# A kernel's written-out order of 948 words is replaced by another of 940

## The chip, the cores and the metric

The kernel runs on one core of a Trainium2 chip. The metric is the device time of one execution in microseconds. Before the change it is 148.19 us, the median of three runs (147.37 to 148.43).

## The reference

Four sequences of 768 steps with 8 heads of 48 channels pass through a linear attention whose state decays by w at every step; the result, 3072 rows of 384, goes through a hidden layer of 1024.

```python
for t in range(S):                       # S = 768, for each of 4 x 8 (batch, head)
    cur = outer(u * k[t], v[t])          # 48 x 48
    y[t] = r[t] @ (state + cur)
    state = w[t][:, None] * state + outer(k[t], v[t])
x = y, heads side by side                # 3072 x 384
h = x @ w_in                             # 3072 x 1024
solu = h * softmax(h)
ln = (solu - mean) / sqrt(var + 1e-6) * g_ln
out = ln @ w_out                         # 3072 x 384
```

## The kernel before

**Tiling.** Steps are cut into 6 chunks of 128. A unit is one chunk of one sequence with all 8 heads; units 0 to 3 are the first chunk of the four sequences, unit 23 is the last. A unit's state depends on the unit four before it.

**One unit.** Four loads of 192 KB bring w, k, r and v (`LW`, `LK`, `LR`, `LV`; functions `load_w` to `load_v`, lines 263 to 273). `lw` takes the logarithm of w on ACT, `cum` sums it along time with two products on PE, `ex` makes exponentials on ACT in place, and `kp` multiplies them with k and r on DVE. `krk` and `krr` turn the scaled k and r by four transposes each on PE, and `kr` copies them out of PSUM; or `kt` (line 398) turns both by one DMA transpose on SP. `M` are the scores, `m` their copy (DVE with the mask, or ACT, and then `sel` masks on GpSimd). `p`, `q`, `qh`, `dg`, `dv` make the bonus of the current step: products on GpSimd (`p` = k r, `q` = p u, `dv` = v dg) and a sum on DVE (`dg`). `vb` casts v. `Y` is the attention's result, `y` its copy; `S`, `et`, `st` carry the state on. `X` turns y by three transposes on PE and `xT` copies it, or `xt` (line 401) does both by DMA. `H` is the hidden product, `e` its exponential on ACT, `he` the product of both on DVE, `hq` its square on ACT, `ea` the sum of the two halves of e on GpSimd. `Oa` and `Ob` are the first and second half of the output product, with one column for the mean and one-column products for the sums of e (of `ea`, if the unit has it) and of hq. `sq`, `qm`, `lv`, `rs` make the scale, `o` applies it, `out` stores 192 KB.

**By rows.** A unit that has the word `ht` (line 404) lays its hidden layer out by rows: six matmuls of 512 columns instead of 24 of 128, sums by the engines' accumulators (two more short readings on ACT and one short square, `sv`) instead of one-column products, and a DMA transpose that turns `he` back. The last unit does its hidden layer in two halves (`HA` to `QB`).

**Weights.** `LI` and `LO` load w_in (three parts of 512 KB) and w_out (two of 768 KB); `wi` casts, `gw` multiplies by g_ln, `mn` makes the column mean, and `ce` subtracts it. `H` needs the first, `Oa` all of them. `hot` issues products of no use that keep PE warm.

**What sets the order.** The string `ORDER` (lines 21 to 68) is the whole schedule. Each word is one stage of one unit, and what follows the dot is an engine (a: ACT, d: DVE, p: GpSimd, which the profile calls POOL), a PSUM bank, or for a load the queue that issues it (none: SP, a: ACT, g: GpSimd). The words are issued from left to right, and `InOrder` (line 73) ties each instruction to the one before it on its engine. So each engine runs its own words in the order of the string and waits where an operand isn't there; between engines nothing is fixed but data. SP is one such queue: a store that waits for `o` or a transpose that waits for `kp` holds up all loads behind it. Buffers come in rings: 7 of each input, 10 of lw and vb, 6 of kp, kr and dv, 4 of most others; a load of unit i waits until unit i - 7 is used.

```python
    for word in ORDER.split():
        word, _, how = word.partition(".")
        name = word.rstrip("0123456789")
        stages[name](int(word[len(name):]), how)
```

All instructions are recorded under line 89, that of the helper, and so are told apart by their tiles.

Of the kernel before, what the change touches and what calls it, by code (L numbers as in the profile page):

```python
# [18 lines left out]


ORDER = """
LR2.a LW0.a LW5 LW2 LV2.g LU0.a LW1.a LK2 LK0.a LW4 LR5 LK5 LV6.g lw2 hot10.0 cum2.0 lw0 cum0.6 LV3.g us0.3
lw5 ex2 kp2 LG0.a ik0 LR0.a cum5.0 uc0 krk2.2 LK1.a LV5.g ih0 ex0 LR1.a krr2 p2 kr2.d q2 qh2 p0 hot3.3 M2.2 q0
LK4 LR4 ex5 dg2 m2.d lw1 hot4.4 cum1.4 LV0.a kp0 vb2.a hot1.2 S2.2 dv2 krk0.3 p5 dg0 p1 lw4 ex1 LW3 cum4.6 kp5
LW6 vb0.p gs0.0 LV1.a dv0 q1 et2 kp1 krr0 ex4 LR3.a kr0.d krk1.1 krr1 LK3.a gc0 kp4 st2 M0.3 kr1.a lw3 vb6.a
LO0.a m0.d hot1.5 M1.6 krk4.2 krr4 LR6 LK6 Y2.i5 vb1.a q5 cum3.3 m1.d lw6 qh1 S1.0 krk5.1 vb5.a cum6.6 dg1
kr4.d S0.2 et1 ex3 ex6 LI0.a kp3 LO1 et0 y2.a krr5 LV4.g LW7 LR7 p3 Y0.i4 dv1 q3 qh3 p4 Y1.n3 y0.a st1 st0
krk3.0 hot1.2 M4.4 kr5.d p6 q4 vb4.p krr3 vb3.a LW8 LK7 kp6 y1.d hot1.1 X1.6 kr3.a LI1.a wi0.p m4.d gw2.a
gw0.a gw1.a dg3 LI2.a gw3.a krk6.0 X2.2 krr6 xT2.d S3.7 et3 gw4.a S5.4 xT1.d dv3 M5.2 S4.1 kr6.d gw6.a et4
M3.5 m5.d q6 X0.0 gw5.a M6.2 et5 xT0.a gw7.a wi1.a m3.d st4 LV8.g wi2.a mn0.5 qh5 lw7 dg4 Y3.i0 dv4 st3 m6.d  # L30
y3.a mc0 dg5 ce2.d ce5.d st5 ce4.d H1.6 LV7.g X3.3 ce7.d xT3.d e1 H0.0 cum7.2 LK8 LW11 LW9 LV9.g he1 lw8 H3.4
e0 he0 H2.6 ex7 e3 S6.0 ce3.p LR11 kp7 he3 ce1.p LR8 ce0.p hq0.a krk7.3 ce6.p Y4.n1 e2 hq1.a et6 ea0.p ea3.p
krr7 y4.d dv5 he2 lw11 st6 Oa0.2 cum8.4 ex8 Ob0 ea1.p kr7.d sq0 LR9 cum11.6 X4.0 ex11 p8 LK11 LR10 qm0 lv0
Oa1.1 lw9 Y5.i3 p7 kp8 rs0 LK10 LW10 M7.4 q7 Ob1 xT4.d kp11 hq3.a y5.a sq1 krk8.0 krk11.6 vb8.p o0.d dg6 LK9
m7.a X5.7 LW12 qm1 krr11 out0 lv1 ea2.p LR12 lw10 vb7.p cum9.2 LV11 xT5.d sel7 q8 dg7 kr11.d rs1 o1.d ex9 krr8
kp9 lw12 H5.4 cum10.6 kr8.d ex10 Oa3.1 p10 e5 hq2.a dv6 kp10 H4.2 cum12.6 Ob3 he5 out1 LK12 dg8 Oa2.0 ex12 sq3
dv7 qm3 e4 p9 vb9.p LV12 lv3 hq5.a ea4.p kp12 S8.4 he4 krk10.5 q9 et8 rs3 Ob2 sq2 M8.6 krr10 LW14 LR14 Y7.n3
vb11.p krk12.2 dv8 o3.d LK14 qm2 lw14 m8.a lv2 st8 S7.1 krk9.4 cum14.6 LW13 y7.d krr12 krr9 kr10.d rs2 out3
et7 vb12.p p11 st7 o2.a ex14 Y6.n0 hq4.a S9.1 et9 kr9.d Oa4.5 q11 LK17 out2 kp14 M9.3 M10.6 Ob4 LW17 kr12.a
LW15 X7.2 sel8 st9 ea5.p y6.d S11.0 m9.a m10.d p12 sq4 xT7.a qm4 M11.3 lv4 M12.1 LR17 et11 rs4 dg9 dv9 sel9  # L40
lw17 Y8.n6 Oa5.7 LV10 m11.d o4.a st11 LK15 cum17.4 Ob5 m12.a y8.d ex17 q10 X6.3 sq5 dg11 vb10.p lw13 q12 qm5
out4 xT6.a lv5 lw15 kp17 LK13 rs5 krk14.0 S12.1 X8.6 xT8.d krr14 LR13 o5.a dg10 cum13.2 LR15 dv11 et12 H6.4
kr14.d out5 st12 ex13 cum15.6 e6 LW16 p14 H7.0 kp13 p13 dv10 ex15 he6 LV15 ea6.p H8.2 LK16 kp15 e7 S10.4 Y9.n5
hq6.a he7 krk15.7 Y10.n6 LW18 lw16 LV16 e8 krr15 et10 y9.d y10.d LR16 M14.0 sel12 Oa6.5 he8 vb15.p X9.6 Ob6
m14.a xT9.d ea7.p LW21 hq7.a sq6 q13 lw18 kr15.d cum16.2 st10 Y11.n6 H9.0 qm6 y11.d M15.6 dg12 ex16 ea8.p
Oa7.4 lv6 rs6 o6.a e9 p15 qh13 LR18 dv12 q14 kp16 LK18 hq8.a m15.d krk16.2 X11.3 vb16.a Ob7 krr16 sq7 he9
cum18.5 q15 p16 out6 dg13 qm7 ex18 p18 lv7 Y12.n7 LK21 LW19 Oa8.0 X10.1 rs7 o7.a y12.d lw21 LR21 kp18 Ob8
xT10.d ea9.p sq8 xT11.d X12.4 S15.7 cum21.5 LK20 out7 lw19 qm8 xT12.d lv8 dg15 dg14 rs8 dv15 q16 ex21 H11.3
# [622 lines left out]
```

## Time and profile before

| | |
|---|---|
| median of 3 runs | 148.19 us |
| profiled execution | 148.38 us |
| its span, first to last instruction | 146.7 us |
| mean granted clock of PE | 0.976 |
| HBM read and written | 22.03 MB, 4.72 MB |
| DMA, mean over the span | 208 GB/s |
| first cumulative sums on PE | 6.17 us |
| last weight landed | 33.3 us |
| first half of the first output | 42.7 us |
| last PE instruction ended | 142.1 us |

The profile is of one execution. Busy shares are those of each engine (PE is TensorE's products, PEld its weight loads); where a line gives a wait, it names what ended it. Small differences between times in the trace are good to a few hundredths of a microsecond, sums of means to about one.

### The profile page before, as it was taken

How to read it: one execution, taken by the hardware profiler on the slowest of the kernel's cores; microseconds unless marked ns; L12 is line 12 of the kernel's file. 1: busy time of each engine (PE TensorE's matmuls, PEld its weight loads, DVE VectorE, ACT ScalarE, POOL GpSimd, SP SyncE). 2: the span in 40 equal slices, each digit the busy share in tenths (PEclk: the TensorE clock that was granted, in tenths of full speed). 3: DMA queues.
4: the chain of work that ended last, by engine and by line, in shares of the span. 5: the costliest groups of instructions: out<-in, count | busy, mean ns of one | idle time of the engine just before them, and what ended most of it. 6: DMA issues, size and time to landing. Idle time of an engine off the chain costs nothing.

```text
span 146.7 us, 4751 instructions
## 1 busy us (share of the span) xinstructions
PE 129.6 (88%) x1847; PEld 96.0 (65%) x1851; DVE 122.5 (84%) x221; ACT 121.9 (83%) x262; POOL 117.7 (80%) x153
## 2 busy tenths in 40 slices
...
GB/s 94 282 295 259 259 261 399 350 352 202 250 173 187 162 222 211 220 203 198 219 138 244 178 243 164 221 189 206 204 182 167 153 197 117 210 190 112 206 107 107
DMA packets 111160, 30.56 MB, mean 208 GB/s; under 512 B 106265, under 2 KB 110370, under 8 KB 111138
## 3 DMA queue, kind: packets, MB, share of 16 engines
...
q10 hardware_dynamic: 12418, 4.53, 11.4%
q0 software_dynamic: 512, 1.57, 3.4%
q8 instruction: 14, 0.23, 0.6%
q14 instruction: 8, 0.07, 0.1%
HBM read 22.03 MB, written 4.72 MB: 182 GB/s over the span
## 4 chain that ended last, share of the span: by engine, by line
PE 33%; DMA 27%; ACT 15%; DVE 10%; POOL 6%; issue 6%; SPq 2%; DVEq 0%; ACTq 0%
PE ps L89 33%; DMA wout_f<-in_moe_w_out_dram 7%; DMA w_in<-in_w_dram 6%; DMA v_in<-in_v_dram 6%; DMA kr_in<-in_k_dram 5%; DVE kp L89 3%; DMA kr_in<-in_r_dram 3%; DVE he L89 2%; ACT ps L89 2%; POOL ea L89 2%; SPq L89 2%; ACT o L89 2%; ACT w L89 1%; POOL m L89 1%; ACT e L89 1%
## 5 line engine op out<-in xcount | busy, mean ns | idle before, releaser
L89 PE MATMUL ps<-w,he 128*128 128x385 bf16 x192 | 43.0, 325 | 0.1
L89 DVE TENSOR_TENSOR kp<-ps,kr_in 128x768 bf16<-128x768 f32 x24 | 22.8, 952 | 6.8 <-ACT ps L89 6.2
L89 PE MATMUL ps<-xT,win_sb 128*128 128x128 bf16 x456 | 28.3, 219 | 0.2 <-ACT win_sb L89 0.2
L89 PEld LDWEIGHTS <-win_sb 128*128 128x128 bf16 x456 | 26.3, 98 | 2.9 <-issue 1.5
L89 ACT ACTIVATE e<-ps 128x1024 bf16<-128x1024 f32 (+1 forms) x25 | 24.5, 985 | 1.6 <-PE ps L89 1.5
L89 PE MATMUL ps<-one_col,hq 128*128 128x1 bf16 x152 | 25.0, 164 | 0.6 <-ACT et L89 0.5
L89 POOL TENSOR_TENSOR p<-kr_in 128x384 bf16<-128x384 f32 x24 | 23.7, 1000 | 1.8 <-DMA kr_in<-in_r_dram 1.7
L89 POOL TENSOR_TENSOR ea<-e 128x512 bf16<-128x512 bf16 x18 | 20.8, 1153 | 5.4 <-ACT e L89 5.4
L89 DVE TENSOR_TENSOR he<-ps,e 128x1024 bf16<-128x1024 f32 (+1 forms) x20 | 23.0, 1164 | 1.4 <-ACT e L89 1.4
L89 ACT ACTIVATE ps<-ps 128x768 f32<-128x768 f32 x24 | 19.3, 805 | 3.3 <-PE ps L89 1.8
L89 POOL TENSOR_TENSOR q<-p,u_bc 128x384 bf16<-128x384 bf16 x24 | 21.7, 911 | 0.3
L89 PEld LDWEIGHTS <-he 128*128 128x128 bf16 x192 | 18.0, 96 | 5.9 <-DMA he<-win_f 0.6
L89 POOL TENSOR_TENSOR dv<-vb,dg 128x384 bf16<-128x384 bf16 x24 | 19.9, 831 | 0.7 <-DVE dg L89 0.4
L89 DVE TENSOR_TENSOR m<-ps,keep 128x1024 bf16<-128x1024 f32 x16 | 19.3, 1218 | 1.1 <-PE ps L89 1.0
L89 ACT ACTIVATE hq<-he 128x1024 bf16<-128x1024 bf16 x18 | 19.0, 1053 | 0.0
L89 PEld LDWEIGHTS <-kp 128*128 128x128 bf16 x208 | 13.8, 102 | 3.0 <-issue 0.6
L89 PEld LDWEIGHTS <-hq 128*128 128x128 bf16 x152 | 11.4, 96 | 6.3 <-ACT hq L89 0.7
L89 ACT ACTIVATE lw<-w_in 128x384 bf16<-128x384 f32 x24 | 12.4, 523 | 3.7 <-DMA w_in<-in_w_dram 3.7
L89 PEld LDWEIGHTS <-kr 64*128 64x128 bf16 (+1 forms) x272 | 10.7, 97 | 6.3 <-issue 2.9
L89 DVE TENSOR_REDUCE dg<-q 128x8 f32<-128x384 bf16 (+1 forms) x24 | 11.4, 478 | 2.9 <-POOL q L89 1.9
L89 PE MATMUL ps<-ident,kp 128*128 128x128 bf16 x128 | 12.7, 234 | 0.2 <-DVE kp L89 0.2
L89 PE MATMUL ps<-inv_col,ea 128*128 128x1 bf16 x72 | 11.9, 165 | 0.0
...
## 6 DMA issues: line engine op xcount, KB each, us to landing
...
```

The costliest lines, as they stand in the source:

```text
L89: made = make(*args, **kwargs)
```

## The change

Only the string `ORDER` changes: the engines, the banks and the places of the words. The code of the stages stays. Counted by words:

| | before | after |
|---|---|---|
| loads of v issued by GpSimd | 8 | 11 (units 10, 11, 12 added) |
| k and r turned by DMA (`kt`) | 8 units: 13, 17 to 23 | 10: 12, 13, 15, 17 to 23 |
| y turned by DMA (`xt`) | unit 23 | 16, 19, 20, 23 |
| hidden layer by rows, turned by DMA (`ht`) | 17 to 21 | 18, 20, 21 |
| `kr` copies on DVE, ACT | 13, 3 | 11, 3 |
| `xT` copies on DVE, ACT | 16, 7 | 13, 7 |
| `o` on DVE, ACT | 11, 13 | 13, 11 |
| `vb` on GpSimd, ACT | 14, 10 | 15, 9 |
| `ea` on GpSimd | 18 | 16 |
| `gw` on ACT, GpSimd | 8, 0 | 7, 1 |
| `ce` on DVE, GpSimd | 4, 4 | 3, 5 |
| warm-up products of `hot` | 21 | 32 |
| u loaded by | ACT | SP |

Which units take which of two engines changes for other words too, without changing the counts (`m` with `sel`, `y`, `wi`, `qh`), and the banks and the order are others throughout. Shown are the start, the lines with the added GpSimd loads, and the stretch from `Ob9` to the end:

```diff
--- before.py
+++ after.py
@@ -19,52 +19,50 @@
 
 
 ORDER = """
-LR2.a LW0.a LW5 LW2 LV2.g LU0.a LW1.a LK2 LK0.a LW4 LR5 LK5 LV6.g lw2 hot10.0 cum2.0 lw0 cum0.6 LV3.g us0.3
-lw5 ex2 kp2 LG0.a ik0 LR0.a cum5.0 uc0 krk2.2 LK1.a LV5.g ih0 ex0 LR1.a krr2 p2 kr2.d q2 qh2 p0 hot3.3 M2.2 q0
-LK4 LR4 ex5 dg2 m2.d lw1 hot4.4 cum1.4 LV0.a kp0 vb2.a hot1.2 S2.2 dv2 krk0.3 p5 dg0 p1 lw4 ex1 LW3 cum4.6 kp5
-LW6 vb0.p gs0.0 LV1.a dv0 q1 et2 kp1 krr0 ex4 LR3.a kr0.d krk1.1 krr1 LK3.a gc0 kp4 st2 M0.3 kr1.a lw3 vb6.a
...
-et15 o8.d kp21 hq9.a kr16.d e11 H12.0 e12 LV14 LW20 st15 H10.5 q18 he11 Oa9.2 Y15.n7 out8 LV13 Ob9 ea11.p he12
-kt13 vb14.a e10 LK19 hq11.a qh16 sq9 he10 lw20 qm9 lv9 vb13.p y15.d Oa11.4 rs9 o9.a p17 M16.0 hq12.a LV17 dv13
-ea12.p M13.5 Ob11 sel14 m13.d X15.2 LR19 sq11 S13.7 Y13.n3 q17 xT15.a cum19.5 qm11 out9 ea10.p lv11 Oa12.2
-rs11 et13 m16.d o11.a y13.d st13 S14.1 ex19 et14 LR20 kp19 dv14 Ob12 X13.7 S16.0 cum20.4 hq10.a LW22 st14 dg18
-p19 Y14.n1 out11 xT13.a sq12 p20 kt18 et16 kt17 lw22 qm12 lv12 st16 rs12 o12.a dg16 out12 H13.6 ex20 dv16 e13
-p21 y14.d vb17.a dg17 kp20 Y16.n1 H15.2 e15 LW23 he13 Oa10.5 LK22 q20 X14.4 y16.d xT14.d Ob10 he15 hq13.a sq10
-S17.4 M17.6 M18.0 lw23 qm10 et17 H14.2 dv17 lv10 rs10 ea13.p st17 m17.a X16.4 LV19 q19 o10.d hq15.a e14 sel17
-LR22 LV18 m18.d out10 Oa13.7 ea15.p xT16.d LK23 LR23 vb18.p he14 cum22.0 q21 ex22 H16.5 Ob13 Y17.n4 Oa15.2 e16
-dv18 kp22 cum23.0 he16 y17.d vb19.a S19.3 hq14.a kt19 dg20 LV20 Y18.n6 qh21 sq13 X17.5 ex23 qm13 kp23 ea14.p
-kt20 qh19 Ob15 y18.d xT17.a lv13 M19.4 kt21 vb20.a sq15 rs13 p23 dg21 H17.0 qm15 o13.a m19.d et19 X18.7 st19
-Oa14.6 M20.4 lv15 p22 e17 out13 xT18.d ea16.p rs15 dg19 S18.3 Ob14 m20.a sq14 he17 dv20 LV21 M21.4 sel20 o15.d
-qm14 kt22 m21.d H18.0 hq16.a dv19 vb21.p Y20.n2 lv14 et18 rs14 dv21 Y19.n7 st18 kt23 q22 q23 y20.d o14.a y19.d
-out14 out15 e18 Oa16.4 Y21.n3 X19.7 X20.6 he18 hq17.a xT20.d Ob16 M22.0 sq16 xT19.a M23.5 LV22 y21.d m22.d
-m23.a qm16 H20.2 X21.5 e20 dg22 vb22.p dv22 xT21.d lv16 sv17 sel23 LV23 H19.6 vb23.p ht17 dg23 Y22.n5 sv18
-ht18 H21.0 dv23 he20 y22.d Oa17.2 rs16 e19 he19 sv20 Y23.n3 hq20.a o16.d hq18.a Ob17 e21 sq17 Oa18.7 X22.4
-hq19.a y23.d xT22.d qm17 ht20 Ob18 sq18 he21 H22.3 qm18 lv17 rs17 lv18 ht19 o17.d rs18 o18.d Oa20.0 e22 xt23
-out16 hq21.a Oa19.1 Ob20 sq20 ht21 he22 qm20 sv21 ea22.p HA23.5 Ob19 lv20 sv19 rs20 hq22.a out18 sq19 EA23
-o20.d qm19 lv19 rs19 HB23.4 out17 DA23 o19.a out20 QA23.d Oa21.2 EB23 Oa22.6 Ob21 Oa23.1 sq21 Ob22 qm21 DB23
-lv21 QB23.d rs21 o21.a out19 out21 sq22 qm22 Ob23 lv22 sq23 qm23 rs22 lv23 rs23 o22.d o23.a out22 out23
+LV6.g LW0.a LR2.a LW2 LU0 LW5 LK0.a LV3.g lw0 LV2.g hot10.0 cum0.1 LK2 LR0.a lw2 LW3 LG0.a LR3.a hot1.0 cum2.3 ex2
+ik0 LV4.g us0.0 ex0 uc0 kp2 LV5.g p2 hot5.5 krk2.6 krr2 LW1.a kp0 q2 lw3 gs0.4 hot1.0 cum3.2 LK3.a lw5 gc0 LK1.a
+kr2.d p0 M2.5 dg2 cum5.0 krk0.4 ex5 LK5 vb2.p dv2 krr0 LR5 m2.d kr0.d ih0 q0 kp5 hot2.5 M0.6 Y2.i4 ex3 LW4 LR1.a
+kp3 lw1 dg0 m0.d LR4 LK4 hot2.0 cum1.0 krk5.5 vb5.p krr5 krk3.2 y2.a krr3 X2.3 kr5.d vb3.a xT2.d kr3.d LV1.a ex1
+vb4.a lw4 LV0.a hot3.4 cum4.6 LW6 LO0.a kp1 p3 LK6 p5 hot3.4 M3.2 q5 ex4 p1 S2.4 krk1.0 vb1.a lw6 krr1 q1 kp4 kr1.a
+m3.d krk4.1 q3 qh1 LI2.a krr4 dg3 dg1 hot1.5 M1.5 vb0.a S1.0 p4 et2 cum6.2 q4 dv0 m1.d hot2.7 S0.6 et1 dv1 ex6
...
+et5 gw2.a wi2.a m5.d st0 dg4 y3.d dg5 xT0.a gw6.a M4.4 gw1.a hot1.2 S4.3 LW8 dv5 y1.d dv4 wi1.p X1.2 m4.d xT1.d
+krk6.0 LK8 krr6 LV7.g gw7.p S3.7 S6.5 et4 LK7 gw5.a gw0.a et3 LV10.g wi0.a LV9.g LW7 LR8 X3.2 kr6.d st5 Y5.i4 gw4.a
+st4 LV8.g st3 M6.0 Y4.i3 et6 H0.6 m6.d xT3.d mn0.0 st6 y4.a y5.a lw8 e0 cum8.2 X5.1 lw7 mc0 ex8 ce0.d ce7.d cum7.4
...
+p10 he2 cum11.3 kr8.d qm0 dv6 lv0 lw9 rs0 kp10 sq3 LR9 dg7 krk7.1 Oa1.5 cum9.6 krr7 qm3 o0.d Ob1 ex11 LV11.g kp11
...
+dg9 out2 LV12.g xT6.a sq4 lw15 kt12 qm4 lv4 ea5.p rs4 st7 X7.5 LR15 H6.3 xT7.d et8 dg11 o4.d vb9.p ex14 p12 q12
...
+dg15 he12 hq11.a S13.4 q18 Oa9.7 cum19.0 M13.5 Ob9 ex19 vb14.a S15.3 sq9 m13.d et13 qm9 st13 LW22 q17 LK19 kp19
+dv15 kt17 Oa11.2 ea12.p Y13.n6 lv9 p19 LW20 et15 y13.d LR21 Y15.n5 y15.d Ob11 S14.1 rs9 dv14 LV17 o9.a out9 hq12.a
+sq11 qm11 lw21 st15 lv11 LV16 ea10.p X13.5 vb17.p rs11 o11.d hq10.a xT13.d lw20 dg17 LK21 sel16 out11 M17.6 Y14.n0
+Oa12.4 X15.5 Ob12 vb16.p cum21.2 m17.a y14.d dg16 H13.6 sq12 dg18 lw22 dv17 Oa10.0 dv16 qm12 ex21 sel17 kt18 et14
+st14 X14.1 lv12 e13 Ob10 kp21 q19 xT15.a ea13.p rs12 M18.2 xT14.a he13 LV18 sq10 LK20 o12.d S17.5 Y17.n1 cum20.6
+m18.a sel18 LR20 Y16.n4 qm10 lv10 y17.d LK22 et17 rs10 H15.2 vb18.p dv18 o10.d ex20 cum22.0 hq13.a y16.d st17 H14.4
+kp20 S16.6 e15 LW23 ex22 he15 p20 q20 LR22 out12 kp22 qh20 Oa13.7 lw23 e14 out10 xt16 hq15.a cum23.2 Ob13 p21 et16
+sq13 he14 qm13 LR23 Y18.n0 y18.d X17.1 xT17.d H16.4 st16 LK23 ex23 hq14.a kp23 e16 H17.0 lv13 ea15.p ea14.p q21
+LV20 he16 X18.2 Oa14.6 LV19 rs13 e17 vb20.a kt19 Oa15.3 p23 ea16.p hq16.a Ob14 M19.4 o13.d sq14 Ob15 vb19.p dg20
+kt21 kt20 he17 qm14 lv14 q23 xT18.d rs14 o14.a hq17.a m19.d sq15 dv20 dg21 out13 dg19 Oa16.0 M21.1 M20.4 m20.d kt22
+ea17.p kt23 m21.a qm15 H18.6 e18 dv19 lv15 p22 Y19.n1 y19.d sel21 out14 q22 Y20.n4 LV21 y20.d rs15 Oa17.2 he18
+vb21.p LV23 Ob16 xt19 dv21 o15.a sq16 Ob17 qm16 dg23 lv16 rs16 sq17 M23.3 qm17 M22.6 LV22 m23.d o16.a S18.1 Y21.n5
+vb22.p lv17 rs17 vb23.a m22.a hq18.a y21.d S19.0 out15 H19.3 xt20 sel22 et18 dv23 et19 o17.d X21.2 sv18 H20.5 out16
+dg22 ht18 st19 e19 xT21.a out17 st18 Y23.n7 H21.1 he19 y23.d dv22 xt23 e20 ea19.p Oa18.4 he20 hq19.a Y22.n0 e21
+Ob18 Oa19.3 y22.d hq20.a ht20 X22.0 Ob19 he21 sq18 sv20 xT22.a qm18 lv18 ht21 H22.0 rs18 HA23.5 Oa20.2 sq19 qm19
+lv19 rs19 o18.d sv21 o19.d e22 he22 EA23 hq21.a hq22.a Oa21.3 out18 Ob20 sq20 ea22.p DA23 Ob21 qm20 QA23.d HB23.1
+lv20 Oa22.4 sq21 rs20 EB23 qm21 Oa23.6 lv21 out19 rs21 Ob22 o21.a sq22 o20.d DB23 QB23.d qm22 Ob23 out20 lv22 rs22
+sq23 out21 qm23 lv23 o22.d out22 rs23 o23.a out23
 
 NIO, NLW, NKP, NWK, NHT = 7, 10, 6, 4, 4
```

More of the change, by code (lines that the diff above doesn't have):

```diff
@@ L21 @@
 ORDER = """
-LR2.a LW0.a LW5 LW2 LV2.g LU0.a LW1.a LK2 LK0.a LW4 LR5 LK5 LV6.g lw2 hot10.0 cum2.0 lw0 cum0.6 LV3.g us0.3
-lw5 ex2 kp2 LG0.a ik0 LR0.a cum5.0 uc0 krk2.2 LK1.a LV5.g ih0 ex0 LR1.a krr2 p2 kr2.d q2 qh2 p0 hot3.3 M2.2 q0
-LK4 LR4 ex5 dg2 m2.d lw1 hot4.4 cum1.4 LV0.a kp0 vb2.a hot1.2 S2.2 dv2 krk0.3 p5 dg0 p1 lw4 ex1 LW3 cum4.6 kp5
-LW6 vb0.p gs0.0 LV1.a dv0 q1 et2 kp1 krr0 ex4 LR3.a kr0.d krk1.1 krr1 LK3.a gc0 kp4 st2 M0.3 kr1.a lw3 vb6.a
-LO0.a m0.d hot1.5 M1.6 krk4.2 krr4 LR6 LK6 Y2.i5 vb1.a q5 cum3.3 m1.d lw6 qh1 S1.0 krk5.1 vb5.a cum6.6 dg1
@@ L27 @@
[L27 to L46, printed above, removed]
@@ L47 @@
-cum18.5 q15 p16 out6 dg13 qm7 ex18 p18 lv7 Y12.n7 LK21 LW19 Oa8.0 X10.1 rs7 o7.a y12.d lw21 LR21 kp18 Ob8
-xT10.d ea9.p sq8 xT11.d X12.4 S15.7 cum21.5 LK20 out7 lw19 qm8 xT12.d lv8 dg15 dg14 rs8 dv15 q16 ex21 H11.3
-et15 o8.d kp21 hq9.a kr16.d e11 H12.0 e12 LV14 LW20 st15 H10.5 q18 he11 Oa9.2 Y15.n7 out8 LV13 Ob9 ea11.p he12
-kt13 vb14.a e10 LK19 hq11.a qh16 sq9 he10 lw20 qm9 lv9 vb13.p y15.d Oa11.4 rs9 o9.a p17 M16.0 hq12.a LV17 dv13
-ea12.p M13.5 Ob11 sel14 m13.d X15.2 LR19 sq11 S13.7 Y13.n3 q17 xT15.a cum19.5 qm11 out9 ea10.p lv11 Oa12.2
@@ new lines @@
+vb4.a lw4 LV0.a hot3.4 cum4.6 LW6 LO0.a kp1 p3 LK6 p5 hot3.4 M3.2 q5 ex4 p1 S2.4 krk1.0 vb1.a lw6 krr1 q1 kp4 kr1.a
+m3.d krk4.1 q3 qh1 LI2.a krr4 dg3 dg1 hot1.5 M1.5 vb0.a S1.0 p4 et2 cum6.2 q4 dv0 m1.d hot2.7 S0.6 et1 dv1 ex6
+Y1.n7 st2 st1 dv3 M5.4 Y0.i0 LI1.a et0 LR6 kp6 gw3.a qh4 vb6.a kr4.a Y3.n3 LO1 hot1.2 S5.1 y0.a LI0.a X0.0 p6 q6
+et5 gw2.a wi2.a m5.d st0 dg4 y3.d dg5 xT0.a gw6.a M4.4 gw1.a hot1.2 S4.3 LW8 dv5 y1.d dv4 wi1.p X1.2 m4.d xT1.d
+krk6.0 LK8 krr6 LV7.g gw7.p S3.7 S6.5 et4 LK7 gw5.a gw0.a et3 LV10.g wi0.a LV9.g LW7 LR8 X3.2 kr6.d st5 Y5.i4 gw4.a
```

14 lines of the change are left out of this document (added).

## The prediction

> **What bounds the kernel now.** I read the page's busy times first, then the stages, the waits, the timeline of the late part, and only then the groups for prices.
>
> ```profile
> PE 129.6 (88%) x1847; PEld 96.0 (65%) x1851; DVE 122.5 (84%) x221; ACT 121.9 (83%) x262; POOL 117.7 (80%) x153
> ```
>
> No engine stands out over the span. The stages 28 to 88, 88 to 118 and 118 us to the end (busy us of PE, PEld, DVE, ACT, POOL; clock; DMA share; GB/s) say more:
>
> ```profile
> 28.00:88.00 60.00, 57.07 (x946) 46.96 (x944) 58.28 (x99) 57.22 (x115) 57.22 (x68) 1.00 0.97 215
> 88.00:118.00 30.00, 28.07 (x453) 21.54 (x451) 25.92 (x43) 26.25 (x57) 26.21 (x30) 1.00 0.99 184
> 118.00:147.00 29.00, 23.89 (x280) 15.83 (x280) 20.34 (x38) 22.60 (x63) 9.73 (x12) 0.99 0.63 155
> ```
>
> In the first stage DVE, ACT and POOL are each 95 to 97% busy: three engines bound at once, and a saving on one alone moves nothing. In the second each loses about 4 us. In the third PE works nearly without a gap until 142.1 us, and POOL has little left. What opens the 4 us is in the waits (total, times, longest):
>
> ```profile
> POOL vb L89 <- DMA v_in<-in_v_dram: 4.5, 2, 2.9
> ACT vb L89 <- DMA v_in<-in_v_dram: 1.5, 1, 1.5
> ```
>
> and in POOL's and PE's timeline (start, duration; in brackets the idle time before and what ended it):
>
> ```profile
> 91.05 0.50 POOL L89 CAST vb<-v_in 128x384 bf16<-128x384 f32 x1 [1.57 <-DMA v_in<-in_v_dram]
> 126.48 0.50 POOL L89 CAST vb<-v_in 128x384 bf16<-128x384 f32 x1 [2.93 <-DMA v_in<-in_v_dram]
> 115.99 0.33 PE L89 MATMUL ps<-ident,y 128*128 128x128 bf16 x3 [1.05 <-ACT o L89]
> ```
>
> v arrives late because SP, one in-order queue, stands behind stores that wait for o:
>
> ```profile
> SPq L89 <- ACT o L89: 6.7, 7, 1.5
> SPq L89 <- DVE o L89: 6.6, 6, 1.9
> ```
>
> So: before 28 us DMA arrival bounds (27 loads of units 0 to 6 land 0.75 us apart until 22.6 us, the weights until 33.3); then three engines together; from about 88 us SP's late loads; from 116 us PE.
>
> **The change, part by part.** Prices, from the groups (count, busy us, mean ns):
>
> ```profile
> L89 POOL TENSOR_TENSOR ea<-e 128x512 bf16<-128x512 bf16 x18 | 20.8, 1153 | 5.4 <-ACT e L89 5.4
> L89 POOL DMA_DIRECT2D v_in<-in_v_dram x8 | 7.4, 923 | 0.0
> L89 POOL TENSOR_TENSOR w<-w,mean_sb 128x384 bf16<-128x384 bf16 x4 | 3.3, 870 | 0.0
> L89 ACT ACTIVATE o<-ps,rs 128x384 f32<-128x384 f32 x13 | 7.5, 580 | 0.3
> L89 ACT ACTIVATE w<-wout_f,gr 128x384 bf16<-128x384 f32 x8 | 4.5, 611 | 0.1
> L89 DVE COPY kr<-ps 128x1024 bf16<-128x1024 bf16 x13 | 8.9, 683 | 1.0 <-PE ps L89 1.0
> L89 DVE COPY xT<-ps 128x384 bf16<-128x384 bf16 x16 | 5.4, 350 | 0.6 <-PE ps L89 0.5
> L89 DVE TENSOR_SCALAR o<-ps,rs 128x384 f32<-128x384 f32 x11 | 6.8, 614 | 0.8 <-ACT rs L89 0.6
> kr<-kp SPq DMA_TRANSPOSE x8, 4.2
> ```
>
> *POOL.* Two `ea` fewer, -2 x 1.153; three loads more, +3 x 0.923; a cast of v, +0.502; a `ce`, +0.870; a `gw`, which POOL has never done here. That one lies between the cast (0.50, one f32 input of the same shape) and `p` (1.00, two); I take 0.6, by the cast. Sum -2.31 + 2.77 + 0.50 + 0.87 + 0.6 = **+2.4 us** (2.3 to 2.8). Counted by words, 1.0 of it stands before Ob16, the 17th second half of an output; the rest lies behind, where POOL has time.
>
> *ACT.* Two `o` (-1.16), a `gw` (-0.61), a cast (-0.51) and two units less by rows, each of which reads two accumulators and squares one column (-2 x (0.200 + 0.196 + 0.191) = -1.17): **-3.4 us**. *DVE.* Two `kr` (-1.37), three `xT` (-1.05), one `ce` (-0.61), two `o` more (+1.23): **-1.8 us**. What is late once they are faster is POOL, which feeds dv, q and the cast v to both: of a saving of 2 to 3 us I count 0.8, between nothing and all of it.
>
> *PE.* 16 + 9 transposes less, 0.056 us from start to start: -1.4. One-column products: 16 of hq and 32 of e more, 8 of ea less, 40 x 0.026 (the step behind each in the timeline): +1.0. Two units' hidden products by 24 matmuls of 128 columns (1.34) for 6 of 512 (1.30): +0.1. Eleven more warm-up products in the start, where PE waits for loads: nothing, at most 11 x 0.24 = 2.6 if they came when work is ready. The total is level, but its place isn't: behind Ob16 the new order has S18, S19 and Y21 (0.46, 0.46, 0.37) and a net -0.15 of other work: **+1.1 us** in the stage in which PE is full.
>
> *The start.* Unit 0's r is the 10th load rather than the 14th, so kp0 starts near 10 us, not at 12.9; but unit 5's is now the 19th, at 4 + 17 x 0.75 = 16.8 us, and kp5 started at 15.4. Units 0 to 6 are the same 28 loads. All weights are queued ahead of units 7 and 8, where w7, r7 and w8 came between: up to -3 x 0.75 = -2.2 us for the last weight, but the new order puts H0 behind S6, Y4 and Y5, by its engines' sums at about the old time. I take -0.3, ends -2 and +1.
>
> *SP.* Three v loads leave (0.62 each, median), u's load comes, and transposes go from 14 to 17, at 1.8 us each from the late ones (14.2 us for eight): +4 us over the span. Queued behind each transpose and store are the next loads, for which POOL (v, k, r), ACT (w, v) and DVE (k, r) wait. From Ob9 to Ob16 SP had 14 loads, 8 transposes, 7 stores; it gets 19, 8 and 6: **+2.5 us** of issue in the very stage where v is late. The cover is slack: SP waits 13.3 us for o in all. With it nothing, without it 2.5. In the forecast I leave it at nothing, since 13.3 us is the larger number. A moved transpose replaces some 0.44 us of PE and 0.68 of DVE by 4.2 us of latency from issue to landing; every one has its own product ordered 2 us or more behind it, by the engines' sums, so that it too is SP's matter.
>
> *The three GpSimd loads.* By the engines' sums, units 10 and 11 are queued 16 to 18 us ahead of their casts and unit 12 some 5 us, so their landing (4.9 us) is covered; what they cost is POOL's 0.923 us each. [...]
>
> **Sum.** POOL paces to Ob16: +1.0; PE from there: +1.1; start -0.3; relief -0.8: **+1.0 us**. The profiled execution took 148.38 us (span 146.7 and 1.7 around it), 0.2 over the median of 148.19. Forecast **149.4 us**, own range 148.0 to 151.0 from the starts' ends, POOL's and half the SP bound. Under 1% (1.5 us) this kernel's measurement can't tell from no change.
>
> **Rivals.**
>
> *Relief decides (0.26).* If ACT and DVE, not POOL, pace the middle, their savings count. Up to Ob16 ACT's words sum to 4.5 us less, DVE's to 2.2 less (part of it moved behind); with +1.1 for PE that is -3.4 or -1.1, and with the start 144.7 or 147.0; I take 145.9. For it: ACT and DVE were as busy as POOL. Against: POOL's idle time in 28 to 88 us is 2.8, a third of it one wait for a weight, and it gets more to do. It decides once POOL has more than 1.0 us to spare before Ob16.
>
> *SP's loads come later (0.25), slower.* One mechanism: in the stretch Ob9 to Ob16 the five added loads put SP 2.5 us later, v and k, r land late by that, and POOL and then PE stand. It decides from the point at which SP's waits for o fall under 2.5 us there. 149.4 + 2.5 = 151.9. For it: v is already late by 1.6, 1.5 and 2.9 us. Against: SP still waits for o in that stage.
>
> [...]
>
> *Nothing moves (0.07).* The orders differ but the same arrivals and the same total of PE (-0.3) decide: 148.2.
>
> **How the numbers follow.** Forecast 0.40: of it 0.23 within 1%, 0.16 slower, 0.01 faster. Relief: 0.24 faster, 0.02 within. SP and GpSimd: 0.27 slower. Nothing moves: 0.06 within, 0.01 faster. Faster 0.26, same 0.31, slower 0.43. The range reaches from the middle of the relief case to just over the SP case: 145.2 to 152.6.
>
> **What would show it.** Right: POOL busy near 120 us with under 3 us idle between 28 and 88; ACT near 118.5, DVE near 120.7; the 17th output's second half ending about a microsecond later; PE full from there. POOL's `gw` row gives the unseen price. The relief case would show POOL waiting for ACT less than the 5.4 us of `ea<-e`, and Ob16 by 120 us. The SP case would show waits of `vb` for v_in above 6 us in sum and POOL idle over 4 us in 88 to 118. I am wrong altogether if the start moves by more than 2 us: then kp6 no longer starts near 26 us.

## The result, and the profile after

The new order is slower: 153.84 us median of 4 runs (152.48 to 155.25), against 148.31 (147.37 to 149.08) for before beside it; the ratio is 1.0346, 95% interval 1.0245 to 1.0446. The profiled execution took 153.94 us (span 152.2), 5.6 more than the one of before. The experiments ran on several chips, on which before's own median lay between 147.92 and 149.64 us, so they are compared by their ratio to before on the same chip; 0.01 is 1.5 us. Executions in a slower state of the chip are left out of the ratios, among them after's of 155.25 us, three of start_of_after's four and the profiled one of before_fill.

The busy times of after (all instructions stand under the helper's line, 89 in before, 87 in after, 88 in some experiments):

```profile
PE 133.5 (88%) x1913; PEld 98.8 (65%) x1913; DVE 121.3 (80%) x217; ACT 121.1 (80%) x252; POOL 120.7 (79%) x157
```

The stages 28 to 88, 88 to 118 and 118 us to the end (columns as before: PE, PEld, DVE, ACT, POOL, clock, DMA share, GB/s):

```profile
28.00:88.00 60.00, 56.00 (x896) 46.15 (x896) 54.95 (x93) 54.91 (x109) 55.69 (x67) 0.97 0.94 209
88.00:118.00 30.00, 28.40 (x469) 22.64 (x467) 25.73 (x44) 27.08 (x54) 27.58 (x32) 1.00 0.97 190
118.00:153.00 35.00, 27.14 (x364) 18.77 (x362) 22.49 (x40) 24.58 (x65) 14.24 (x17) 0.97 0.59 145
```

Two things stand out. In the first stage every engine has lost 1.1 to 3.3 us of busy time and the granted clock reads 0.97 where it read 1.00. In the last stage TensorE is idle for 7.9 of 35 us (5.1 of 29 in before); 5.3 and 4.9 of these lie behind its last product, so while it has work it stands for some 2.6 us against 0.2. The waits (total, times, longest):

```profile
POOL ea L87 <- ACT e L87: 8.8, 3, 5.8
POOL vb L87 <- DMA v_in<-in_v_dram: 6.3, 3, 2.5
PE ps L87 <- DMA kr<-kp: 2.4, 3, 1.1
SPq L87 <- DVE o L87: 13.9, 6, 5.9
SPq L87 <- ACT o L87: 2.5, 7, 0.6
```

and the groups that answer to the prices of the prediction:

```profile
L87 POOL DMA_DIRECT2D v_in<-in_v_dram x11 | 10.1, 920 | 0.0
L87 POOL TENSOR_SCALAR w<-wout_f,gr 128x384 bf16<-128x384 f32 x1 | 1.3, 1268 | 0.0
```

**Where the 5.6 us went.** A word of the order has a price on TensorE: its matmuls, each at its usual time from one start to the next, which is short of its length in the timeline because matmuls overlap (in after the 24 of H0, 0.22 us long each, take 1.35 us from the first one's start at 35.28 us to the next word's at 36.63). Take the start of a word and subtract the prices of all words ahead of it on TensorE (warm-ups not counted): that is TensorE's lag, the time that it has stood or run slowly so far. The differences between the columns are what counts; with the median of these times they come out the same to 0.1 or 0.2 us, while the columns themselves move by up to 0.9. From the two traces, and from two of the experiments below, in us:

| at (us) | before | after | he0_first | four_pe |
|---|---|---|---|---|
| 38 | 20.3 | 21.1 | 21.2 | 20.8 |
| 46 | 21.5 | 25.0 | 22.7 | 22.2 |
| 102 | 24.1 | 26.2 | 25.1 | 24.0 |
| 118 | 25.7 | 28.7 | 26.4 | 26.5 |
| 134 | 26.1 | 32.0 | 29.3 | 27.0 |

After loses 3.5 us against before up to 46 us, of it 2.7 between 38 and 46; it wins 1.4 back up to 102; and loses 3.8 again behind 102 us, 2.9 of them between 118 and 134. So there are two losses at two places and a gain between them.

**The first place.** The timelines of TensorE and DVE in after (start, length; in brackets the idle time ahead):

```profile
41.03 5.81 PE L87 MATMUL ps<-xT,win_sb 128*128 128x128 bf16 x72 [2.11 <-DVE he L87]
```

```profile
38.71 1.14 DVE L87 SCALAR_TENSOR_TENSOR w<-wout_f,gr,ps 128x384 bf16<-128x384 f32 x2 [1.86 <-ACT mean_sb L87]
39.76 1.22 DVE L87 TENSOR_TENSOR he<-ps,e 128x1024 bf16<-128x1024 f32 x1
```

H3 goes into the bank of H0, which he0 has to read first. On DVE he0 stands behind two centrings (ce0, ce7), and these wait 1.86 us for the mean, which ScalarE copies at 38.16 us, behind an exponential and a logarithm. TensorE stands for 2.11 us. What follows is in the stages of 3.41 us around it (TensorE's busy time, clock, DMA share, GB/s):

```profile
38.14:41.55 3.41, 1.30 (x17) 1.00 1.14 290
41.55:44.96 3.41, 3.41 (x36) 0.50 0.97 195
44.96:48.37 3.41, 3.41 (x56) 1.00 1.06 209
```

Right behind the gap the clock reads 0.50 for 3.41 us, and the 72 matmuls of H3, H1, H2 take 5.81 us.

**The second place.** Three of TensorE's waits between 92 and 136 us; in before TensorE has no wait for kr, xT or vb there:

```profile
PE ps L87 <- DMA kr<-kp: 1.9, 2, 1.1
PE ps L87 <- DMA xT<-y: 0.9, 1, 0.9
PE ps L87 <- POOL vb L87: 0.7, 1, 0.7
```

The waits for kr are those of the scores of units 18 and 19, and these two are turned by DMA in before as well. Their sources were ready at 83.1 and 95.9 us (83.5 and 96.8 in before), but SP came to kt18 at 101.2 and to kt19 at 114.0 us, 5.2 and 5.9 us later than in before, while TensorE itself was 2 to 3 us behind. Only the wait for xT, 0.9 us ahead of H20, is the landing of a transpose that the change had added; vb is GpSimd's cast of v21.

Two theories were set against each other. S+L (its second half is Theory SP further on): the loss at the start is he0's wait and the clock, the late loss is SP's list. Rival P, later Rival A: the engines' pace sets the end wherever one begins, so neither matters. The results, ratio to before and interval:

| kernel | ratio | interval |
|---|---|---|
| after | 1.0346 | 1.0245 to 1.0446 |
| start_of_before | 1.0454 | 1.0382 to 1.0526 |
| late_of_before | 1.0615 | 1.0558 to 1.0673 |
| he0_first | 1.0197 | 1.0139 to 1.0255 |
| warm_fill | 1.0167 | 1.0096 to 1.0237 |
| tail_order | 1.0254 | 1.0182 to 1.0325 |
| tail_pe | 1.0162 | 1.0085 to 1.0238 |
| tail_both | 1.0171 | 1.0065 to 1.0277 |
| out_later | 1.0116 | 1.0032 to 1.0200 |
| all_pe | 1.0124 | 1.0042 to 1.0205 |
| after_late_g | 1.0139 | 1.0074 to 1.0205 |
| all_pe_late_g | 1.0273 | 1.0203 to 1.0343 |
| four_pe | 1.0069 | 1.0019 to 1.0119 |
| four_pe_stores | 1.0141 | 1.0072 to 1.0209 |
| before_turned | 1.0665 | 1.0553 to 1.0776 |
| before_loads_g | 1.0026 | 0.9971 to 1.0081 |
| before_fill | 1.0095 | 1.0047 to 1.0143 |
| before_late_g | 1.0003 | 0.9954 to 1.0052 |

### The profile page after: what moved, and what is told of

It is laid out like the page before. It is cut to its first block, busy times and chain, and to the rows that moved or that the text cites. A ratio compares the mean times of both kernels' runs of the same rounds, so it can differ in the third digit from the quotient of the medians.

```text
span 152.2 us, 4862 instructions
## 1 busy us (share of the span) xinstructions
PE 133.5 (88%) x1913; PEld 98.8 (65%) x1913; DVE 121.3 (80%) x217; ACT 121.1 (80%) x252; POOL 120.7 (79%) x157
## 3 DMA queue, kind: packets, MB, share of 16 engines
q0 software_dynamic: 704, 2.16, 4.9%
## 4 chain that ended last, share of the span: by engine, by line
PE 49%; DMA 25%; DVE 12%; SPq 4%; ACT 3%; POOL 2%; issue 2%; ACTq 0%; DVEq 0%; POOLq 0%
PE ps L87 49%; DMA w_in<-in_w_dram 7%; DMA kr<-kp 7%; DMA v_in<-in_v_dram 6%; SPq L87 4%; DVE kp L87 4%; DMA kr_in<-in_r_dram 3%; DVE m L87 3%; DMA xT<-y 2%; DVE he L87 2%; DVE dg L87 1%; POOL vb L87 1%; POOL dv L87 1%; DVE kr L87 1%; ACT ps L87 1%
## 5 line engine op out<-in xcount | busy, mean ns | idle before, releaser
L87 PE MATMUL ps<-xT,win_sb 128*128 128x128 bf16 x504 | 32.5, 225 | 2.5 <-DVE he L87 2.5
L87 PEld LDWEIGHTS <-win_sb 128*128 128x128 bf16 x504 | 30.5, 101 | 3.9 <-issue 2.9
L87 DVE TENSOR_TENSOR he<-ps,e 128x1024 bf16<-128x1024 f32 (+1 forms) x22 | 25.7, 1171 | 3.1 <-ACT e L87 3.1
L87 PE MATMUL ps<-one_col,hq 128*128 128x1 bf16 x168 | 27.5, 164 | 0.0
L87 POOL TENSOR_TENSOR ea<-e 128x512 bf16<-128x512 bf16 x16 | 18.5, 1157 | 8.8 <-ACT e L87 8.8
L87 ACT ACTIVATE hq<-he 128x1024 bf16<-128x1024 bf16 x20 | 21.0, 1052 | 1.0 <-DVE he L87 0.9
L87 PEld LDWEIGHTS <-hq 128*128 128x128 bf16 x168 | 13.3, 96 | 6.9
L87 DVE TENSOR_TENSOR y<-ps,dv 128x384 bf16<-128x384 f32 x20 | 10.7, 551 | 2.6 <-PE ps L87 1.3
L87 POOL CAST vb<-v_in 128x384 bf16<-128x384 f32 x15 | 7.5, 503 | 6.3 <-DMA v_in<-in_v_dram 6.3
L87 PE MATMUL ps<-ident,kp 128*128 128x128 bf16 x112 | 9.8, 226 | 2.5 <-POOL p L87 1.9
```

Source lines behind the costliest of these rows:

```text
L87: made = make(*args, **kwargs)
```

## Experiments: the two orders spliced

Each takes the words of one order up to a point and what is then missing in the order of the other.

```diff
 start_of_before: 308 words of before (to cum10.6 ahead of kr8.d), then after
 start_of_after:  304 words of after (to sq1 ahead of qm1), then before
 late_of_before:  586 words of after (to he12 ahead of hq11), then before
```

> The first 308 words in the order of before (to about 51 us), the rest in the order of after; one bank moved (H4 to bank 6). Theory S+L: after loses in two places, 3.4 us by Ob0 (he0 stands on DVE behind two centrings, TensorE is idle 2.1 us, the granted clock then reads 0.5 for 3.4 us) and 3.8 us behind 92 us (SP's loads and transposes late), and gains 1.3 us between them. Then this kernel runs at 153.8 - 3.4 = 150.4 us (149.9 to 151.0) and the clock shows no second fall at 41 us. Rival P (the pace of the middle, not the start, sets the end, and time won at the start is waited away later): 153 to 154 us.

> The first 304 words in the order of after (to about 52 us), the rest in the order of before; one bank moved (M7 to bank 1). Theory S+L: 148.3 + 3.4 = 151.7 us (151.0 to 152.2), with TensorE idle about 2 us near 39 us and the clock at 0.5 behind it. Rival P: the loss of the start is taken up in the slack of before's middle, 148.3 to 149.3 us.

> The first 586 words in the order of after (to about 91 us), the rest in the order of before, no bank moved. Theory S+L: the late 3.8 us are gone, 153.8 - 3.8 = 150.0 us (149.5 to 150.8), and DVE's waits for k and r and GpSimd's for v behind 92 us are as short as in before. Rival P: the late part follows whatever comes before it, 153 us or more.

Measured: 1.0454 and 1.0615 for the first and third, both slower than after itself; for the second there is one execution, 150.09 us beside 147.92 for before, 2.2 us more, between the two expectations. The splices did not isolate anything, because the seam costs more than the parts. In start_of_before TensorE stands 1.6 and 1.2 us at 54 and 60 us, in late_of_before 2.6 and 1.6 us at 92 and 96 us, where the words of the one order find the work of the other not ready. The clock falls besides: in late_of_before for 6.83 us from 96.14, in start_of_before at 35.13 us, among words that are before's own and had the full clock there. An order of words is no sum of its stretches. From here on single words were moved.

## Experiments: the start

```diff
-... y4.a y5.a lw8 e0 cum8.2 X5.1 lw7 mc0 ex8 ce0.d ce7.d cum7.4 he0 dg6 ...
+... y4.a y5.a lw8 e0 he0 cum8.2 X5.1 lw7 mc0 ex8 ce0.d ce7.d cum7.4 dg6 ...
```

> After with one word moved: he0 ahead of ce0 and ce7 on DVE (beside e0), so that the product for H3's bank no longer stands behind the two centrings that wait for the mean on ScalarE. Theory S+L: the 2.1 us of idle TensorE at 38.8 us go (1.9 of them, the wait of ce0 for the mean), the clock stays at 1.0 there (1.7 us: 72 matmuls in 4.0 instead of 5.65 us), 153.8 - 3.6 = 150.2 us (149.7 to 151.0). If the idle stretch goes and the clock falls all the same: 151.9 us. Rival P: 153 to 154 us.

Measured: 1.0197 (150.90 us on its chip), nearer to the theory; by the ratios one moved word wins 2.2 us against the 3.6 expected (the intervals of after and of this kernel together leave 0.5 to 3.9). In its trace TensorE's idle time ahead of H3 and the stage in which the clock fell (timeline, then the stage):

```profile
39.33 1.50 PE L87 MATMUL ps<-xT,win_sb 128*128 128x128 bf16 x24 [0.24 <-DVE he L87]
41.70 2.84 PE L87 MATMUL ps<-xT,win_sb 128*128 128x128 bf16 x48 [0.87 <-DVE kp L87]
```

```profile
38.37:41.79 3.42, 2.31 (x33) 1.00 1.19 306
41.79:45.20 3.41, 3.41 (x59) 1.00 0.88 184
```

The clock stays at 1.00, and the next work, Oa0, starts at 44.38 instead of 46.68 us: 2.3 earlier, not 3.6, since TensorE now waits 0.87 us for kp there. Of these 2.3 us the lag shows 1.1 at 102 us, 2.3 again at 118 and 2.7 at 134: part of the gain is waited away in the middle and shows again behind it. The time stays under the 153 us of Rival P (152.1 at the interval's upper end), which falls.

Which part was the wait, and which the clock?

```diff
-... lw8 e0 cum8.2 X5.1 lw7 ...
+... lw8 e0 cum8.2 hot8.1 X5.1 lw7 ...
```

> After with eight warm-up matmuls of zeros (0.22 us each) in bank 1 ahead of X5: TensorE is kept busy to about 40.5 us, and H3 still starts at 41.0 us behind he0. It tells the clock from the wait. If the fall of the clock to 0.5 at 41.5 us comes of the 2.1 us of idle TensorE, the fall is gone and the 72 matmuls of H3, H1 and H2 take 4.0 us instead of 5.65: 153.8 - 1.7 = 152.1 us, and of the 2.9 us that the moved he0 won, 1.7 were the clock. If the clock falls all the same, or the wait alone carries the loss: 153.8 to 154.2 us.

Measured: 1.0167. The warm-ups fill the gap, H3 starts when it did in after, and the same 72 matmuls are faster:

```profile
38.32 1.89 PE L87 MATMUL ps<-warm 128*128 128x512 bf16 x8
41.04 4.18 PE L87 MATMUL ps<-xT,win_sb 128*128 128x128 bf16 x72 [0.34 <-DVE he L87]
```

4.18 instead of 5.81 us: the clock alone, 1.6 us here. Over the whole kernel it wins as much as moving he0 (intervals overlap, the lags at 134 us are 29.4 and 29.3). So the idle 2.1 us cost little by themselves, at most about 1 us by the two intervals; most of what stayed in the time was the clock's fall behind them.

The same was tried on before, whose clock falls at 16.75 us behind a gap of 1.65 us.

```diff
-... krk0.3 ... lw4 ex1 LW3 cum4.6 kp5 ...
+... krk0.3 ... lw4 ex1 LW3 hot5.6 cum4.6 kp5 ...
```

> Before with five warm-up matmuls of zeros (1.1 us) in bank 6 ahead of cum4, so that the 1.65 us in which TensorE is idle at 14.8 us, behind which the clock reads 0.5 from 16.75 to 23.58 us, become 0.55. If a gap of 1.6 us is enough to halve the clock, and a shorter one isn't, the fall goes; TensorE is busy nearly throughout those 6.8 us, and the time falls by 0.5 to 2.5 us: 145.8 to 147.8 us. If the fall comes all the same (of the work before it, or of the gap of 0.9 us ahead of it): 148.3 to 149.0 us. If the start waits for its loads and not for TensorE: the clock stays and the time is 148.0 to 148.5 us.

Measured: 1.0095, above all three cases. The mean clock of the seven executions in its ratio was 0.960 to 1.000 (before's: 0.969 to 0.988), so some of the falls did go; but the execution with 1.000, in which the clock never fell, took 150.93 us, and two with 0.994 took 149.59 and 150.69. In its trace the fall behind the filled gap is gone, but there is one at 8.62 us and one of two steps at 32.52. With the warm-ups in it the kernel is 0.7 to 2.1 us slower (by the interval), fall or no fall, and its executions at 0.986 and above (149.50 to 150.96 us) are little faster than those at 0.960 and 0.974 (151.08 and 150.95). In these few executions the fall is worth about a microsecond or less to before, where it cost after more than two; that before's start waits for its loads and not for TensorE would explain this, but it is argued.

## Experiments: the late part

All of these start from he0_first (1.0197). First only SP's list, no instruction more or less:

```diff
-... kt20 ... out13 ... kt22 ... kt23 ... out14 ... LV21 ... LV23 ... xt19 ... LV22 ... xt20
+... kt20 LV21 LV23 LV22 ... kt22 ... kt23 ... xt19 xt20 out13 out14
```

> The kernel with he0 ahead of the centrings (150.9 us), and in it only SP's list behind kt20 in another order: the loads of v for 21, 23, 22 ahead of kt22, the transposes xt19, xt20 right behind y19, y20, and the stores out13, out14 behind them. No instruction more or less on any engine. Theory SP (SP issues without a gap from 92 to 132 us, so what it has late in its list comes late): vb21 starts near 122.5 instead of 125.2 us, H19 near 125 instead of 126.4, 150.9 - 2.0 = 148.9 us (148.3 to 149.6). Rival A (the late loss is on DVE, ScalarE or GpSimd themselves, the loads wait for nothing that matters): 150.4 to 151.2 us.

Measured: 1.0254, no gain; both theories expected less. The loads of v came in time (vb no longer waits there), but kt22 and kt23 stood behind them. TensorE's wait between 118 and 134 us, and the stages:

```profile
PE ps L87 <- DMA kr<-kp: 2.3, 2, 2.0
```

```profile
122.06:125.47 3.41, 1.39 (x27) 1.00 1.07 143
125.47:128.88 3.41, 3.41 (x52) 0.50 0.82 274
```

One late arrival was exchanged for another, 2.0 us in one piece, and the clock fell behind it (M23, for kt23). SP issues here for 37.0 of the 40 us between 92 and 132 us in after (32.0 in before): whatever is put ahead makes something else late.

Then work was taken off SP.

```diff
 tail_pe: two transposes back on TensorE
-... xt19 ... xt20 ...
+... he18 X19.1 xT19.d ... Ob17 X20.5 qm16 xT20.d ...
 tail_both: tail_order and tail_pe together (out13, out14 behind kt23)
 out_later: tail_pe, and three stores later on SP
-... out0 ... out3 ... out1 ... LW15 ...
+... LW15 out0 out3 out1 ...
```

> The kernel with he0 ahead of the centrings (150.9 us), and in it xt19 and xt20 taken from SP and done as in before: three PE transposes each, into banks 1 and 5, and a DVE copy each. Theory SP: two transposes of 1.25 to 2.8 us leave SP's list, the loads LV22 behind xt19 lands 2.8 us earlier, H19 and H20 wait for no landing: 150.9 - 1.5 = 149.4 us (148.8 to 150.2), TensorE pays 0.3 us. Rival A: 150.9 + 0.3 to + 0.8 = 151.2 to 151.7 us.

> Both of the last two together (the v loads ahead, out13 and out14 behind kt23, xt19 and xt20 on TensorE). Theory SP: the two overlap, 148.5 us (147.8 to 149.3), little better than the order alone. Rival A: 151 to 151.7 us.

> After with he0 ahead of the centrings and X19, X20 on TensorE (150.5 us), and the stores out0, out3, out1 behind LW15 on SP. SP stands at out0 from about 44 to 51 us there and is full from 60 us to 132; behind those stores stand LV11, LK9, LW12, LW14, LW13, LK12, LR12, LR14. Theory SP: SP begins 3 to 6 us earlier with what it needs the whole late part for, and as far as rings let it, the late waits for v and k shrink: 149.3 us (148.8 to 150.0). Rival A: nothing, 150.3 to 151 us.

Measured: 1.0162, 1.0171 and 1.0116. Each interval overlaps that of he0_first; tail_pe's won 0.5 us where 1.5 were expected, tail_both 0.4 where 2.4 were, and out_later won 0.7 on tail_pe where 1.2 were. None of them decides alone.

```diff
 all_pe: out_later, and kt12, kt15, xt16 back on TensorE (krk, krr, kr.d; X, xT.d)
 after_late_g: out_later with three loads of v on GpSimd
-... LV21 ... LV23 ... LV22 ...
+... LV21.g LV22.g vb17.p ... q23 LV23.g ...
 all_pe_late_g: both
```

> After with he0 first, X19 and X20 on TensorE and three stores later (1.0116 of before), and now kt12, kt15 and xt16 on TensorE as well: none of the change's five added transposes by DMA is left. Theory SP: three more transposes of 1.25 to 2.8 us leave SP's list, the waits for v, k and kr in the stretch 92 to 125 us shrink: 1.0116 - 0.003 to - 0.010 = 1.002 to 1.009 of before. Rival A (the pace of ScalarE, DVE and TensorE counts, the five transposes were a relief): 1.012 to 1.020.

> The same base (1.0116 of before), with LV21 and LV22 issued by GpSimd in the 1.9 us in which it waits for v17 near 98 us, and LV23 behind q23; SP has three loads less in the late part. Theory SP: the waits of GpSimd and ScalarE for v21, v22, v23 (2.7, 0.2 and 0.75 us) go, and what stands behind these loads on SP comes 1.5 us earlier: 1.000 to 1.007. Rival A: 1.010 to 1.018; and if GpSimd sets the pace there, its 2.8 us more make it 1.018 to 1.03.

> Both of these. Theory SP: 0.996 to 1.004 of before. Rival A: 1.012 to 1.022.

Measured: 1.0124, 1.0139, 1.0273. By the numbers the first two are Rival A's, and the third is slower than either expected. For the loads there is more than the numbers: in after_late_g GpSimd waits 0.2 us in all for v (6.3 in after), and the ratio is 0.0023 above out_later's. The theory's gain of 0.7 us and more did not come; a smaller one is not excluded, since the 0.7 us that TensorE waits for vb in after are gone from this trace too. What TensorE waits for there is a transpose by DMA, kt18 again (timeline):

```profile
103.26 0.40 PE L87 MATMUL ps<-kr 64*128 64x128 bf16 x8 [2.16 <-DMA kr<-kp]
```

All_pe holds two opposite effects. Between 110 and 140 us its lag grows by 1.8 us less than tail_pe's; but it has 1.9 us more near 66 us, where the copy of kr12 stands behind he6 on DVE:

```profile
65.52 0.62 PE L88 MATMUL ps<-ident,kp 128*128 128x128 bf16 x8 [0.62 <-DVE st L88]
67.25 0.62 PE L88 MATMUL ps<-kr 64*128 64x128 bf16 x16 [1.11 <-DVE kr L88]
```

All_pe_late_g has both kinds of wait in its trace, 2.0 us for kt18 and the two near 66 us. So the last two kernels leave kt12 with SP:

```diff
 four_pe: out_later, and kt15, xt16 back on TensorE (X16, xT16.d; krk15, krr15, kr15.d)
 four_pe_stores: the same, out0, out3, out1 where after has them
```

> After with he0 first, three stores later, and xt16, xt19, xt20 and kt15 on TensorE; kt12 stays with SP. Theory SP (the added transposes of the late part cost it 1.8 us, and the last kernel without them lost as much near 66 us to its own copy of kr12): 1.0124 - 0.012 = 1.000 of before (0.995 to 1.006). Rival A (the late part costs what it costs): 1.010 to 1.015.

> The same with out0, out3 and out1 where after has them, so that SP stands at out0 near 45 to 50 us. Theory SP: SP comes 3 us later to the loads of 9 to 14, which waits of 0.3 to 0.6 us may show: 1.003 (0.997 to 1.010). Rival A: as the other, 1.010 to 1.015.

Measured: 1.0069 and 1.0141. The first lies just outside the range of the theory and below that of Rival A; with he0_first its interval no longer overlaps (1.0119 against 1.0139). The second is in Rival A's range, and its interval overlaps both that of four_pe and that of he0_first, so the transposes without the stores are not resolved. The stretch 118 to 136 us of before, after, tail_pe and four_pe (TensorE's busy time is the first number behind 18.00):

```profile
118.00:136.00 18.00, 17.78 (x213) 11.70 (x214) 16.39 (x28) 16.25 (x43) 9.73 (x12) 1.00 0.79 170
```

```profile
118.00:136.00 18.00, 15.45 (x217) 10.19 (x216) 14.08 (x23) 13.39 (x33) 13.09 (x16) 1.00 0.81 180
```

```profile
118.00:136.00 18.00, 17.36 (x252) 12.26 (x249) 14.56 (x28) 15.30 (x40) 9.79 (x12) 1.00 0.72 163
```

```profile
118.00:136.00 18.00, 17.73 (x259) 12.77 (x260) 15.33 (x28) 16.02 (x42) 10.56 (x13) 1.00 0.62 147
```

With transposes back on TensorE it is as full as in before, for the most part with xt19 and xt20 alone (he0_first, without these, has 15.64 us). The 2.3 us that TensorE stood there in after came of SP's list: the landing of xt20, kt19 behind its place, and v. Of the 0.0346, 0.0149 are he0's word, 0.0128 (about 0.005 to 0.02) the four transposes and three stores together, and 0.0069 (0.0019 to 0.0119, about 1.0 us) stays open. The trace of four_pe has a place for it: at 107.9 us X16 stands for 1.87 us, because kp22, which still reads its bank, waits 1.18 us for r22 from SP. The lag is 0.1 under before's at 102 us and 0.8 over it at 118. Another bank for X16 was not tried. No version beat before.

## Experiments: parts of the change alone, in before

```diff
 before_turned: kt12, kt15, xt16, xt19, xt20 in place of krk, krr, kr and X, xT
 before_loads_g: LV10, LV11, LV12 on GpSimd
 before_late_g: LV20, LV22, LV23 on GpSimd
-... LV20 ... LV22 ... LV23 ...
+... LV20.g sel17 ... LV22.g LV23.g sel20 ...
```

> Before with one part of the change alone: kt12, kt15, xt16, xt19 and xt20 turned by SP's DMA in place of TensorE's transposes (8 x 2 and 3 x 3 of them) and their five copies; all else in its order. Theory SP (SP's list is what the late part of after waits for; a transpose takes 1.25 to 2.8 us of it): SP in before is busy 6.1 to 7.4 of every 8 us from 60 us on and gets 6 to 9 us more, so later loads come late: 148.3 + 1 to + 2.5 = 149.3 to 150.8 us. Rival A (SP's fullness costs nothing, the relief of the engines counts): TensorE -1.3 us, DVE and ScalarE -1 each: 147.0 to 148.0 us.

> Before with another part alone: the loads of v for 10, 11 and 12 issued by GpSimd (LV10 behind LV9, the two others where they stood) in place of SP. GpSimd pays 3 x 0.92 = 2.8 us, SP is relieved of 3 x 0.5. The forecast of this study counted GpSimd's pace in full: +0.5 to +2 us, 148.8 to 150.3. Theory SP: GpSimd's 2.8 us are found again in its own waits (5 to 9 us of idle in the stretch), and SP has 1.5 us less: 147.6 to 148.5 us.

> Before with LV20, LV22 and LV23 issued by GpSimd in its own idle time (0.9 us ahead of sel17, 1.9 us ahead of sel20) in place of SP. In before ScalarE waits 1.5 us for v20 and GpSimd 2.9 us for v22 behind 112 us. Theory SP (late loads set the late part of before too): 0.990 to 0.997 of before, faster than both kernels. If those waits end beside TensorE's own: 0.998 to 1.002. If GpSimd's pace decides: 1.004 to 1.015.

Measured: 1.0665, 1.0026 and 1.0003. The five transposes alone cost before about 9.9 us, four times the theory's upper end. SP takes its list in order: kt12 was issued at 59.31 us, when Y6, the last reader of its buffer, was through (58.9 to 59.5), though kp12 was ready at 55.4, and the loads stood behind it. The waits of before_turned show whom that hit (4.5 and 3.7 us in before):

```profile
POOL vb L87 <- DMA v_in<-in_v_dram: 11.7, 4, 5.7
ACT lw L87 <- DMA w_in<-in_w_dram: 7.0, 4, 3.4
```

In after, the loads were ordered around the transposes; there four of them, with the three stores, cost some 2 us. The two kernels with loads on GpSimd say that three of them are free (under 0.8%, 1.2 us), and that GpSimd's 4.5 us of waits for v in before, which the prediction took for the bound of its late part, end beside something else: with 1.7 of them left in before_late_g the time is the same to 0.5% (0.8 us).

## Why the prediction was wrong, by its steps

**The sum** said +1.0 us, range 145.2 to 152.6; it was +5.5. The direction had the largest chance, 0.43; the size was missed.

**The start** is the step that failed most: -0.3, ends -2 and +1, against +3.5. The loads it was argued from went about as told (kp5 at 16.9 us by the trace, 16.8 by the prediction; kp0 at 12.2, not near 10), and the lag at 38 us is only 0.8 over before's; kp6, whose start the prediction had named as the sign of a moved start, came 1.2 us later (27.3 for 26.1), ahead of the loss. The loss sits in words that the step did not look at: ce0, ce7 and he0 on DVE, and H3's bank. "By its engines' sums at about the old time" priced each engine's list, and H0 did come at the old time (35.3 against 35.9 us); a product waiting for a bank, read by a word that stands behind a wait on another engine, has no term in such sums. Nor had the clock: the prediction read 1.00 for the stage and took it as given. he0_first and warm_fill show that the clock's fall is 1.6 us on the spot and, with what it drags along, 2.2 to 2.7 at the end by the two ratios, which leave 0.5 to 4.5.

**POOL paces to Ob16, +1.0.** The prices held but one: `gw` on GpSimd took 1.268 us, outside the bounds of 0.5 to 1.0 taken from its neighbours. GpSimd is busy for 3.0 us more than in before (+2.4 told). But GpSimd did not pace: it was idle 4.3 us between 28 and 88 us where the step wanted under 3, and before_loads_g put 2.8 us more on it and took at most 1.2 us longer. The step fell.

**ACT -3.4, DVE -1.8, counted as -0.8.** The instructions' lengths sum to 138.1 and 134.6 us, 3.4 and 1.7 less than in before: the prices were right. The sign "ACT near 118.5" was nevertheless wrong (121.1): neighbours on ScalarE overlap in the trace, and the busy time counts the overlap once (lengths of 141.5 us for 121.9 busy in before, 138.1 for 121.1 in after). The lag fell by 1.4 us against before between 46 and 102 us, which fits the relief, a little more of it than was counted; that it was the relief is argued, not shown.

**PE behind Ob16, +1.1.** Ob16 started at 125.4 us, 2.8 later than in before; behind it TensorE was not full but waited, so this term was not what counted.

**SP, left at nothing of 2.5,** is the other step that failed: behind 102 us the lag grew by 3.8 us against before, and 1.9 us came back when four transposes and three stores were taken out of SP's way. The reason given was that SP waits 13.3 us for o in all. That is a sum over the span; of it 4.1 us lie between 92 and 132 us, and SP issues 5.0 us more there than in before. The cover was counted where it wasn't. The rival on SP had the place and about the size (151.9 with no loss at the start), and its sign, waits of vb above 6 us in sum, came true at 6.3; its other sign, GpSimd idle over 4 us between 88 and 118, did not (2.4). Its mechanism was half right: v's late loads came true as a wait, but taking them off SP won nothing that could be measured (after_late_g, before_late_g); TensorE waited for transposes, one of them new and two that stood in before too and were issued 5 to 6 us later. The prediction had said of each transpose that its product is ordered 2 us or more behind it, and rightly concluded that this is SP's matter, but then gave SP no price.

**The three GpSimd loads.** 0.920 us each in after, as priced, and three of them free in before to within 1.2 us. No run shows an issue held up by VectorE, for which 0.02 of the prediction's chances stood, in its 0.27 for "SP and GpSimd": the eight issues in before took 0.88 to 1.05 us; those at 32.30, 34.52 and 35.44 us took 0.92, 0.92 and 0.88, in which VectorE was busy for 0.92, 0.52 and 0.72; the longest of the eleven in after took 1.06.

**Relief decides, nothing moves**: both are excluded by the interval of the ratio.
